# Unit 0's second half activated a place sooner, and step 3's w, v and constants loaded at other places

## The chip, the cores and the metric

The kernel runs on one core of one Trainium2 chip. The metric is device time in microseconds (us) of one execution; lower is better. TensorE (PE in the profile) does the matrix products, VectorE (DVE), ScalarE (ACT) and GpSimd (POOL) the rest, and SyncE (SP) issues most of the transfers from memory. Each engine works through its own queue in the order in which the program wrote it.

## The reference

Two blocks follow each other. The first is a linear attention with decay (batch 4, 8 heads, 768 tokens, head size 48), the second a feed-forward layer on the 3072 tokens with 384 features and 2048 hidden units, whose activation is h * erf(softplus(h)):

```python
for t in range(S):
    cur = np.einsum('bhd,bhe->bhde', u[None] * kt, vt)
    y[:, :, t] = np.einsum('bhd,bhde->bhe', rt, state + cur)
    state = wt[:, :, :, None] * state + np.einsum('bhd,bhe->bhde', kt, vt)
# x = y as (tokens, features)
h = x @ w_in
sp = np.maximum(h, 0.0) + np.log1p(np.exp(-np.abs(h)))
g = h * erf(sp)
return g @ w_out
```

The weights `w_in` and `w_out` come as 64-bit floats and are turned to 32 bits in the kernel.

## The kernel before, in words

**Steps and units.** The work is cut into 12 steps, s = 0 to 11. A step takes 128 tokens of two batches through the attention: it loads r and k (`in`), the decays (`w`) and `v`, multiplies tokens in pairs of blocks that double in size (levels 1 to LOG = 6: `level_products`, L546, makes the products, `scale`, L334, multiplies the decays in for the next level, `take_level`, L558 and L565, picks up what the level gives), and ends with `from_own` (L580), transposes of k (L919, copied by L921), the state (`state_part`, L654, L941 to L946) and `through_state` (L606). That leaves the step's 256 tokens as xT, through the PSUM tile `y` (L613, L633, L634, and rows moved by DMA in L640). From step 4 (`DIRECT`) on, the low levels come from rows instead, which `prepare` works out on VectorE and GpSimd (L469 to L490) with `u_row`, and with `block_sb` in L520.

A unit is the feed-forward work of one step's tokens. `hidden` (L1008) multiplies xT by `w_in` in two halves g = 0 and 1 of four pieces each; a piece fills one of two PSUM banks named m and ScalarE copies it to h (L1017). A half is then activated in three stages: softplus (L990) and erf (L993) on ScalarE, each with a load of its table, and the product with h (L997, two instructions on VectorE). `project` (L1040) multiplies by `w_out`, four f-blocks to a piece; it uses the same two banks.

**What sets the order.** All five queues are written out by hand under a manual schedule. In steps 1 to 3 `attend` calls `place(n)` after each level (n = 0 to 5), after the transposes (6) and at the end (7). A place does up to three things: it converts a block of weights (`convert_at`, with the table `CONVERT`), it runs some activation stages (`advance(STAGES[s][n])`), and it runs a piece or two of a unit (`beside`). In step 2 these are the eight pieces of unit 1, one to a place, after a rest of unit 0's last piece at place 0; in step 3 unit 0 is projected at places 0 to 3 (two pieces to a place) and unit 2 is multiplied at places 4 to 7.

**Activation stages.** The stages stand in one list, `later`, in the order in which the halves became complete. `advance(count)` takes stages from its front; a count of 1 is one stage, 2 is two. With the counts of the kernel before, unit 0's second half gets its softplus at place 7 of step 2, its erf at place 0 of step 3 and its product at place 1, where unit 1's first half also gets its softplus.

**Conversion of the weights.** Block i (two of the 16 f-blocks of `w_in` for i < 8, of `w_out` for i from 8 on) is loaded as two halves of 384 KB into one of three buffers `words` (L147). For `w_out`, ScalarE scales the high words into the PSUM tile `y` (L256) and the low words into `rest` (L262), VectorE shifts `y` (L271) and merges the sign (L276), and GpSimd adds `rest` (L284). A buffer is free again after L276. There is one tile `y`, which the attention uses too. The last three blocks of `w_out` (i = 13 to 15) are converted in step 3 at places 0 to 2.

**Loads.** `load_step(s + 2)` at the end of step s loads the tiles of the step after next. At the end of step 1 it issues for step 3, in this order on SyncE's queue: `in` (L147, 1 MB), `w` (L151, 512 KB), `block_sb` (L198, 32 KB), `u_row` (L199, 24 KB) and `v` (L186, 384 KB), between the weights of block 10 and of block 11. The tiles `w` and `v` have two buffers each, used in turn.

Of the kernel before, what the change touches and what calls it, by code (L numbers as in the profile page):

```python
# [39 lines left out]
DIRECT = 4  # L40
NEAR_LOG = 4
NEAR = 1 << NEAR_LOG
LOG = 6
# [18 lines left out]
def kernel(  # L62
# [14 lines left out]
    nc = tc.nc  # L77
# [40 lines left out]
    block_sb = const.tile([P, HC], FP32, name="block_sb")  # L118

    sums = const.tile([P, NEAR, NEAR], FP32, name="sums")  # L120
    u_row = const.tile([P, D], FP32, name="u_row")
# [22 lines left out]
    def load_halves(dst, src):  # L144

        for i in range(2):
            nc.sync.dma_start(out=dst[:, i], in_=src[:, i])  # L147

    def load_w(s):
        ws[s] = ins.tile([P, JP, C], FP32, name="w")  # L150
        nc.sync.dma_start(out=ws[s][:], in_=rkw[s][:, 2])  # L151
# [31 lines left out]
    def load_v(s):  # L183

        vt = loaded[s][1]
        nc.sync.dma_start(out=vt[:], in_=v[s])  # L186

    def load_step(s):
        t = ins.tile([P, 2, JP, C], FP32, name="in")
        vt = ins.tile([P, NH, D], FP32, name="v")  # L190
        if s < DIRECT:
            load_halves(t, rkw[s])
        else:
            nc.sync.dma_start(out=t[:], in_=rkw[s][:, 0:2])
        if s <= DIRECT:
            load_w(s)
        if s == 3:
            nc.sync.dma_start(out=block_sb[:], in_=block_mask)  # L198
            nc.sync.dma_start(out=u_row[:], in_=u_rows)  # L199
        loaded[s] = t, vt  # L200
        load_v(s)

    def near_log(s):
        return NEAR_LOG - (s == DIRECT)
# [3 lines left out]
    def load_rows(s):  # L208

        rk = wide.tile([P, 2, DM, 2], I32, name="words", bufs=3)  # L210
        rk = rk[:].rearrange("p x n two -> p x (n two)").bitcast(FP32)
        w = wide.tile([P, 2, DM], I32, name="rest", bufs=2)
        w = w[:].rearrange("p x n -> p (x n)").bitcast(FP32)
        nc.sync.dma_start(out=rk, in_=rk_rows[s])
        nc.sync.dma_start(out=w, in_=w_rows[s])
        rows_of[s] = [x.rearrange("p (t n) -> p t n", t=NEAR) for x in (rk[:, 0], rk[:, 1], w)]
# [370 lines left out]
    def fence():  # L587

        nc.vector.tensor_copy(
            out=seen[:].rearrange("p (e g t) -> p e g t", e=NE, g=NP),  # L590
            in_=y[:].rearrange("p e j q t -> p e (j q) t")[..., HC - 1 : HC + 1],
        )
# [95 lines left out]
    def attend_late(s, run):  # L688
# [12 lines left out]
        if before:  # L701
            from_own(before, ready[before][0], 0)
            through_state(before, xTs[before])
            if s + 1 < n_steps:
                load_step(s + 1)
# [140 lines left out]
    def stay_warm(times):  # L846

        for _ in range(times):
            ps = ps_m.tile([P, NC, P], FP32, name="m")
            nc.tensor.matmul(  # L850
                ps[:], lhsT=ident[:], rhs=ident[:, None, :].to_broadcast([P, NC, P]),
                start=True, stop=True,
            )

    def keep_busy(pp, columns=(DM, DM // 2)):

        zeros = states[1][0][:].rearrange("p n d -> p (n d)")
        for n in columns:
# [3 lines left out]
            )  # L862

    def attend(s, xT, early, place, behind):

        c, in_t, vt, made, S, S_next, ends = parts_of(s)
# [280 lines left out]
    def advance(count=None):  # L1147

        while later and count != 0:
            stage, last = later.pop(0)  # L1150
            stage()
            count = count and count - 1
            if last and not count:
                break

    def beside(s, k):


        kind, of, pieces = (projs, s - 3, 2) if k < 4 else (hids, s - 1, 2)
        if s in ALONE:  # L1160
            kind, of, pieces = hids, s - 1, 1
        for _ in range(pieces):
            piece(kind, of)
# [11 lines left out]
    def in_order(s, k):  # L1175


        order = ("APPP", "APPP", "APPHH", "AHHH", "AHHH")
        for what in order[k]:
            if what == "A":  # L1180
                advance()
            elif what == "P":
                piece(projs, s - 3)
            else:
                piece(hids, s - 1)
# [17 lines left out]
    def run_late(s, tokens, following=None):  # L1203

        for what in tokens.split():
            if what == "A":
                advance()
            elif what == "P":
                piece(projs, s - 3)
            elif what == "H":  # L1210
                piece(hids, s - 1)
            elif what == "F":
                next(following, None)
            elif what == "G":
                mixing.send(nc.gpsimd)
            elif what == "s":
                softplus_chunk()
            elif what[0] == "e":
                erf_chunk(what[1])
            elif what == "m":  # L1220
                multiply_chunk()
            elif what[0] == "k":
                to_lane(s - 2, what[1:3], what[3])
            else:
                blend(s - 2, *(int(n) for n in what[1:]))
                if what == "S3":
                    del lanes["11"], lanes["22"]
                elif what == "S4":
                    del lanes["12"]
# [6 lines left out]
    )  # L1236

    STAGES = {
        1: (0, 0, 0, 0, 0, 0, 1, 0), 2: (1, 0, 0, 0, 0, 0, 1, 1), 3: (1, 2, 1, 0, 0, 2, 1, 1)
    }  # L1240
    ALONE = {1, 2}

# [8 lines left out]
    for kk in range(KT):  # L1251
        n = D // KT
# [3 lines left out]
    with tc.manual_schedule(  # L1256
        engines={getattr(mybir.EngineType, x) for x in ("PE", "DVE", "Activation", "Pool", "SP")}
    ):
        stay_warm(6)
        for t in (*states[0], *states[1], middle):  # L1260
            nc.gpsimd.memset(t[:], 0.0)
        nc.gpsimd.memset(over_blocks[:], 1.0)
        nc.scalar.copy(u_row[:, :1], ident[:, :1])
        stages, send = convert(
            [
                (into[:, f : f + 2, :], given[:, f : f + 2, :])
                for into, given in ((w_in_sb, w_in), (w_out_sb, w_out))
                for f in range(0, NT, 2)
            ]
        )  # L1270
        stages["l"](0, loaded[0][0][:, 1, JP - 1, C - 1 : C])
        for s in range(n_steps):
            xTs[s] = xs.tile([P, KT, UNIT], FP32, name="xT")
            places = iter(range(8))

            def convert_at(n, late=True):
                if s < len(CONVERT) and n < len(CONVERT[s]):
                    send(CONVERT[s][n][late])

            def place(n):  # L1280
                if n == LOG - 1 and DIRECT - 1 <= s <= DIRECT:
                    load_rows(s + 2)
                for due in {(3, 4): (5,), (4, 3): (6,), (4, 5): (7,)}.get((s, n), ()):
                    load_w(due)
                if s >= DIRECT:
                    in_order(s, next(places))
                    return
                if s in ALONE:
                    if s == 2 and not n:

                        next(hids[0])
                        turns.pop("ahead")()
                    convert_at(n)
                    if s == 2 and not n:
                        beside(s, next(places))
                        advance(STAGES[s][n])
                        return
                    advance(STAGES[s][n])
                else:
                    advance(STAGES[s][n])  # L1300
                    convert_at(n)
                    if s == DIRECT - 1 and not n:
                        load_rows(DIRECT)
                beside(s, next(places))

            def run(n, following):
                if n == 3 and s < n_steps - 2:
                    load_rows(s + 2)
                if n == 3 and s + 3 < n_steps:
                    load_w(s + 3)  # L1310
                run_late(s, LATE.get(s, USUAL)[STAGES_LATE.index(n)], following)

            if s > DIRECT:
                attend_late(s, run)
                continue
            if s:
                attend(
                    s, xTs[s], lambda n: convert_at(n, False), place, lambda: convert_at(LOG + 2)
                )
            else:  # L1320
                attend_first(xTs[s])
            if s and s + 2 < n_steps:
                load_step(s + 2)
        s = n_steps
        from_own(s - 1, ready[s - 1][0], 1)
        fence()
        run_late(s, "s P")
        from_own(s - 1, ready[s - 1][0], 0)
        through_state(s - 1, xTs[s - 1])
        run_late(s, "m ey m P s P P ep m P P P S H H s H ey m H H s H ep m H H")  # L1330
        run_late(s + 1, "s P ey m P s P P ep m P P P S")
        run_late(s + 2, "P P P P P P P")
# [96 lines left out]
```

## Time and profile before

| what | value |
| --- | --- |
| median of 3 runs | 596.46 us (594.95 to 597.97) |
| profiled execution: its own time | 598.04 us |
| profiled execution: its span | 596.3 us |
| TensorE busy | 583.9 us (98%) |
| VectorE busy | 440.3 us (74%) |
| ScalarE busy | 361.2 us (61%) |
| GpSimd busy | 272.0 us (46%) |
| mean granted clock of TensorE | 0.997 |

The span is the time from the first to the last instruction of the profiled execution; its own time has some 1.7 us around it. In the profile, L1008 is line 1008 of the kernel, and out<-in are tiles by the program's names. "Idle before" is time in which the engine stood still ahead of an instruction, with what it waited for last. Step 1 runs from about 27 to 60 us, step 2 to 96 us, step 3 to 153 us; later steps take some 45 to 50 us each.

### The profile page before, as it was taken

What the parts mean: (1) busy time and instruction counts of PE and PEld (TensorE: products, weight loads), DVE (VectorE), ACT (ScalarE), POOL (GpSimd) and SP (SyncE); (2) the same over time, 40 slices, a digit from 0 to 9 for tenths busy, and PEclk for the clock granted to TensorE, in tenths of its full rate; (3) what the DMA queues carried; (4) which work ended last, traced back from release to release, by engine and by line L of the source; (5) the groups of instructions that cost most, each with busy time, mean ns of one, the idle gap of its engine ahead of it and who ended that gap; (6) DMA issues with size and microseconds to landing.
All of it is one profiled execution on the core that took longest, in us unless ns stands there. A gap on an engine that the chain in (4) does not pass through costs nothing.

```text
span 596.3 us, 16614 instructions
## 1 busy us (share of the span) xinstructions
PE 583.9 (98%) x7264; PEld 500.8 (84%) x7264; DVE 440.3 (74%) x518; ACT 361.2 (61%) x474; POOL 272.0 (46%) x305
## 2 busy tenths in 40 slices
PE   8899999989999999999999999999999999999997
PEld 6687777568768757898898898898898898898997
DVE  6786885998996799799799799799799525023140
ACT  3568867616534398665666666666666664746710
POOL 3456382700588559749449449459459000000000
PEclk9999999989999999999999999999999999999999
DMA  7684672341314324334334334334331300000000
GB/s 239 234 310 163 218 248 79 142 142 20 140 38 154 69 90 168 72 107 169 72 108 168 73 106 169 73 108 132 73 107 53 73 9 26 2 21 13 2 27 27
DMA packets 53937, 63.24 MB, mean 106 GB/s; under 512 B 35144, under 2 KB 40424, under 8 KB 52840
## 3 DMA queue, kind: packets, MB, share of 16 engines
q1 hardware_dynamic: 53480, 61.98, 32.5%
q8 instruction: 57, 0.93, 0.7%
q10 hardware_dynamic: 384, 0.20, 0.1%
q14 instruction: 16, 0.13, 0.1%
HBM read 52.39 MB, written 8.69 MB: 102 GB/s over the span
## 4 chain that ended last, share of the span: by engine, by line
PE 88%; DVE 5%; ACT 3%; DMA 1%; issue 1%; ACTq 0%; POOL 0%; DVEq 0%; SPq 0%; POOLq 0%
PE m L1008 39%; PE m L1116 28%; PE m L1040 8%; PE pp L546 5%; PE y L580 2%; PE pp L654 2%; DVE in L334 2%; PE y L606 2%; DMA words<-in_moe_w_out 1%; PE m L850 1%; PE pp L919 1%; DVE h L997 1%; ACT rest L262 1%; DVE own L558 1%; ACT y L256 1%
## 5 line engine op out<-in xcount | busy, mean ns | idle before, releaser
L1008 PE MATMUL m<-xT,w_in_sb 128*128 128x256 f32 x1152 | 258.6, 383 | 1.5 <-ACT h L1017 1.4
L1008 PEld LDWEIGHTS m<-xT,w_in_sb 128*128 128x128 f32 x1152 | 217.4, 191 | 33.1 <-ACT h L1017 1.6
L1017 ACT COPY h<-m 128x512 f32<-128x512 f32 x96 | 55.5, 580 | 87.5 <-PE m L1008 87.4
L334 DVE TENSOR_TENSOR in<-in,tot_sb 128x1024 f32<-128x1024 f32 (+1 forms) x59 | 82.6, 1400 | 16.4 <-PE pp L546 14.3
L469 POOL TENSOR_TENSOR rk<-words 128x528 f32<-128x528 f32 (+3 forms) x28 | 42.4, 1514 | 91.6 <-DVE sums L459 81.2
L473 POOL TENSOR_TENSOR words<-words,rest 128x528 f32<-128x528 f32 (+10 forms) x77 | 78.2, 1016 | 6.0
L1040 PE MATMUL m<-w_out_sb,h 128*128 128x384 f32 x192 | 64.3, 491 | 0.8 <-DVE h L997 0.8
L1040 PEld LDWEIGHTS m<-w_out_sb,h 128*128 128x128 f32 x192 | 35.7, 190 | 24.5 <-issue 0.9
L1116 PE MATMUL m<-mixed,h 128*128 128x192 f32 x288 | 51.1, 331 | 0.0
L1116 PE MATMUL m<-w_out_sb,h 128*128 128x192 f32 x288 | 50.3, 329 | 0.0
L964 ACT ACT_TABLE_LOAD x36 | 46.2, 1283 | 2.7 <-issue 2.0
L1116 PEld LDWEIGHTS m<-w_out_sb,h 128*128 128x128 f32 x288 | 46.9, 190 | 0.5
L1116 PEld LDWEIGHTS m<-mixed,h 128*128 128x128 f32 x288 | 46.6, 190 | 0.9
L968 ACT ACT_TABLE_LOAD x36 | 46.2, 1283 | 1.7 <-DVE room L1099 1.1
L546 PEld LDWEIGHTS pp<-in 48*64 48x64 f32 (+1 forms) x2368 | 33.4, 126 | 13.6 <-DVE in L334 6.0
L1116 PE MATMUL m<-w_out_sb,room 128*128 128x192 f32 x256 | 44.2, 326 | 0.0
L1116 PEld LDWEIGHTS m<-w_out_sb,room 128*128 128x128 f32 x256 | 42.0, 190 | 0.0
L973 DVE TENSOR_TENSOR h<-h,y 128x1024 f32<-128x1024 f32 x17 | 20.7, 1215 | 28.3 <-ACT y L968 28.2
L546 PE MATMUL pp<-in 48*64 48x64 f32 (+1 forms) x2368 | 37.7, 212 | 3.1 <-DVE in L334 3.1
L964 ACT ACTIVATE room<-h 128x1024 f32<-128x1024 f32 x36 | 38.0, 1057 | 0.4
L973 DVE TENSOR_TENSOR h<-h,pp 128x1024 f32<-128x1024 f32 x19 | 23.0, 1213 | 19.5 <-ACT pp L968 19.5
L469 POOL TENSOR_TENSOR words<-words 128x336 f32<-128x336 f32 (+6 forms) x49 | 35.3, 720 | 3.8
(141 smaller groups left out, 821.7 us busy)
## 6 DMA issues: line engine op xcount, KB each, us to landing
in<-in_rkw SPq DMA_DIRECT2D x8, 1024.0 KB, 5.4
words<-in_moe_w_in SPq DMA_DIRECT2D x16, 384.0 KB, 4.3
words<-in_moe_w_out SPq DMA_DIRECT2D x16, 384.0 KB, 3.5
words<-in_rk_rows SPq DMA_DIRECT2D x8, 768.0 KB, 5.8
w<-in_rkw SPq DMA_DIRECT2D x11, 512.0 KB, 6.9
v<-in_v SPq DMA_DIRECT2D x12, 384.0 KB, 6.3
out<-o SPq DMA_DIRECT2D x24, 192.0 KB, 2.1
in<-in_rkw SPq DMA_DIRECT2D x7, 512.0 KB, 5.3
```

What stands on the lines that cost most here:

```text
L334: nc.vector.tensor_mul(halves, halves, view(tots[level - 1], 0, [[1, n], [2, nb], [0, half]]))
L469: engine.tensor_mul(terms[n], r[:, :, n:], k[:, :, : near - n])
L473: engine.tensor_mul(k[:, :, :m], k[:, :, :m], w[:, :, n : n + m])
L546: nc.tensor.matmul(pp[s0 : s0 + m, e, n, :m], lhsT=rk[rows(e), 1, n, s0 : s0 + m], rhs=rk[rows(e), 0, n, t0 : t0 + m], start=True, stop=True,)
L580: nc.tensor.matmul(y[at(e, p), e, j, p // 2, t], lhsT=vt[t, n * NE + e, :], rhs=own[t, e * JP + n, :], start=swap == 1 and not j and not q ...
L964: nc.scalar.activation(sp_room, chunks[0], AF.Softplus)
L968: nc.scalar.activation(at, sp_room, AF.Erf)
L973: nc.vector.tensor_mul(h, h, at)
L1008: nc.tensor.matmul(ps[:, ff, :], lhsT=w_in_sb[:, g * FG + f + ff, kk * P : (kk + 1) * P], rhs=xT[:, kk, :], start=kk == 0, stop=kk == KT - 1,)
L1017: nc.scalar.copy(h[:, f : f + FT, :], ps[:])
L1040: nc.tensor.matmul(ps[j][:], lhsT=gs[g][:, f, j * C : (j + 1) * C], rhs=w_out_sb[:, g * FG + f, :], start=g + f == 0, stop=g == NG - 1 and ...
L1116: nc.tensor.matmul(to, lhsT=a[:, f], rhs=b[:, f], start=start and f == 0, stop=f == FG - 1, skip_group_check=True,)
```

## The change

The change has two parts. First, the counts of `STAGES`: place 6 of step 2 takes two stages instead of one, and place 1 of step 3 one instead of two. The first stage at place 6 is the product of unit 0's first half, as before; the second is now the softplus of unit 0's second half, ahead of the copy of the piece of that place. Its erf then comes at place 7 of step 2, ahead of the copy there, and its product at place 0 of step 3, ahead of the conversion of block 13. Unit 1's first half is activated at the same places as before. On VectorE, the two L997 instructions of that half move from behind the L558 of level 2 to behind L898 (level 1). On ScalarE, two table loads, softplus and erf move accordingly. The queues of TensorE and GpSimd keep their order.

Second, the loads for step 3 other than `in`. `w` is issued at place 5 of step 1, behind the weights of block 9. `v`, `block_sb` and `u_row`, in this order, are issued at place 4 of step 2, behind the weights of the last block. The weights of block 11 follow directly on `in` of step 3.

```diff
@@ load_step
-        if s <= DIRECT:
+        if s == DIRECT:
             load_w(s)
-        if s == 3:
-            nc.sync.dma_start(out=block_sb[:], in_=block_mask)
-            nc.sync.dma_start(out=u_row[:], in_=u_rows)
         loaded[s] = t, vt
-        load_v(s)
+        if s > 3:
+            load_v(s)
@@ STAGES
-        1: (0, 0, 0, 0, 0, 0, 1, 0), 2: (1, 0, 0, 0, 0, 0, 1, 1), 3: (1, 2, 1, 0, 0, 2, 1, 1)
+        1: (0, 0, 0, 0, 0, 0, 1, 0), 2: (1, 0, 0, 0, 0, 0, 2, 1), 3: (1, 1, 1, 0, 0, 2, 1, 1)
@@ place
                     convert_at(n)
+                    if (s, n) == (1, LOG - 1):
+                        load_w(3)
+                    if (s, n) == (2, LOG - 2):
+                        load_v(3)
+                        nc.sync.dma_start(out=block_sb[:], in_=block_mask)
+                        nc.sync.dma_start(out=u_row[:], in_=u_rows)
```

## Prediction

> **What bounds the kernel now.** I read the shares of busy time first, then TensorE's waits, then its timeline where the waits lie, then the timelines of the engines it waits for.
>
> ```profile
> PE 583.9 (98%) x7264; PEld 500.8 (84%) x7264; DVE 440.3 (74%) x518; ACT 361.2 (61%) x474; POOL 272.0 (46%) x305
> ```
>
> TensorE is busy for 583.9 of 596.3 us, so only its 12.4 us of holes, and any slow stretch in its busy time, can be won. Its waits over the whole run, those that matter (in total, times, longest):
>
> ```profile
> PE pp L546 <- DVE in L334: 3.1, 4, 2.3
> PE m L1008 <- ACT h L1017: 1.4, 2, 1.1
> PE m L1040 <- DVE h L997: 0.8, 1, 0.8
> ```
>
> After 126 us there is no wait on this list. TensorE's timeline (start, duration, idle before):
>
> ```profile
> 80.17 2.86 PE L1008 MATMUL m<-xT,w_in_sb 128*128 128x256 f32 x12 [1.08 <-ACT h L1017]
> 84.03 2.86 PE L1008 MATMUL m<-xT,w_in_sb 128*128 128x256 f32 x12 [0.32 <-ACT h L1017]
> ...
> 110.85 5.40 PE L1040 MATMUL m<-w_out_sb,h 128*128 128x384 f32 x16 [0.78 <-DVE h L997]
> ...
> 117.27 5.43 PE L1040 MATMUL m<-w_out_sb,h 128*128 128x384 f32 x16
> 125.03 1.16 PE L546 MATMUL pp<-in 48*64 48x64 f32 x64 [2.34 <-DVE in L334]
> 126.12 7.13 PE L1008 MATMUL m<-xT,w_in_sb 128*128 128x256 f32 x24
> ```
>
> Four holes lie within reach, 4.52 us: two in step 2 (s=2) behind ScalarE, two in step 3. The last row is a fifth cost: the same 24 matmuls take 5.45 us at 133.87. The table of stretches (clock in the third column from the end) shows why:
>
> ```profile
> 125.00:126.00 1.00, 0.97 (x64) 0.97 (x64) 1.00 (x2) 0.00 (x0) 0.00 (x0) 1.00 0.87 201
> 127.00:128.00 1.00, 1.00 (x4) 0.74 (x3) 0.90 (x4) 0.00 (x0) 0.00 (x0) 0.50 0.99 416
> ```
>
> Right behind the 2.34 us hole the clock is halved for some 3.3 us, which costs 7.13 - 5.45 = 1.68 us. Who makes the hole: VectorE in step 3, without idle from 103.69 on.
>
> ```profile
> 103.69 2.08 DVE L334 TENSOR_TENSOR in<-in,tot_sb 128x1024 f32<-128x1024 f32 x1 [0.97 <-PE pp L546]
> ...
> 108.71 3.97 DVE L997 TENSOR_TENSOR h<-h,room 128x1024 f32<-128x1024 f32 x2
> 112.61 1.63 DVE L334 TENSOR_TENSOR in<-in,tot_sb 128x1024 f32<-128x1024 f32 x1
> ...
> 116.61 2.26 DVE L476 TENSOR_TENSOR words<-words,u_row 128x768 f32<-128x768 f32 x1
> 118.80 1.49 DVE L469 TENSOR_TENSOR rk<-words 128x672 f32<-128x672 f32 x1
> ...
> 123.76 1.22 DVE L334 TENSOR_TENSOR in<-in,tot_sb 128x1024 f32<-128x1024 f32 x1
> ```
>
> The last of these releases TensorE at 125.03; the product of L997, 3.97 us, stands in front of it. And ScalarE, in step 2:
>
> ```profile
> 77.92 0.91 ACT L256 ACTIVATE y<-words 128x768 f32<-128x768 f32 x1 [3.22 <-DMA words<-in_moe_w_out]
> ...
> 91.74 1.28 ACT L990 ACT_TABLE_LOAD   x1
> 93.03 1.91 ACT L990 ACTIVATE room<-h 128x2048 f32<-128x2048 f32 x1
> 95.23 0.59 ACT L1017 COPY h<-m 128x512 f32<-128x512 f32 x1 [0.29 <-PE m L1008]
> ...
> 99.86 0.87 ACT L256 ACTIVATE y<-words 128x768 f32<-128x768 f32 x1 [2.36 <-DMA xT<-y]
> ```
>
> The 3.22 us wait for weights is what pushes the copies of L1017 at 79.54 and 83.39 behind TensorE.
>
> **What the Trainium skill says.** "TensorE: Matmul & The Clock Gate", Part 1, has the clock fall to half after an idle window of about 3.4 us, the window running freely. Here 2.34 us was enough, and holes of 1.08 and 0.78 us cost no clock (1.00 in both stretches). "GPSIMD Engine Reference", section 1, says that GpSimd shares its SBUF interfaces with VectorE's instructions of two SBUF inputs. The trace agrees: L334 takes 1.22 us alone and 2.08 beside an add of L284; L997 takes 2.36 alone (138.59) and 3.97 beside L284 and L408. "DMA: Bandwidth & Descriptors", section "Issuing engines are not separate DMA queues", has all transfers run on the same 16 engines, so bytes issued ahead delay what follows: 308 GB/s moved from 64 to 75 us.
>
> **The change, part by part.**
>
> *The loads of step 3.* w (512 KB), v (384), the block mask (32) and u_row (24) were issued at 66.19 to 68.75, ahead of five loads of weights. w goes to step 1, place 5, behind the weights issued up to 50.44; the engines move 5 to 7 GB/s between 55 and 62, and its buffer was last read near 33. v and the two constants go behind the last weights of step 2 (85.5 before). They are needed at 139 (L580), 151 (L520) and 116.6 (L476), and land near 90: cost nothing, with over 22 us of cover. In SyncE's queue the next after them is xT at 97.25, which waits for ScalarE anyway. What it gives: 952 KB at 308 GB/s are 3.2 us, so the weights that landed at 77.8 land near 74.6. ScalarE is then free at 74.7, but bank y only when L276 ends (74.44 + 0.95), so L256 starts near 75.4: 2.5 us sooner. The copies end near 77.6 and 81.5; TensorE asks at 79.09 and 82.63. Both holes go: 1.40 us.
>
> *The activation.* Softplus of unit 0's second half (1.28 + 1.91) moves ahead of the copy of place 6, erf (the same) ahead of the copy of place 7; no table load is added. With 1.4 us off: the L386/L389 row ends at 89.7, softplus 92.9, copy 93.4, erf 96.6, copy 97.1. TensorE wants the two banks back at 95.7 and 102.1, so 2.3 and 5 us cover it. Late next: the copy of y starts at 97.0 (94.9 if only shifted), the xT rows and step 4's loads behind it go at 100.8 instead of 99.9, and L256 starts at 97.0 + 3.56 = 100.6. xT is needed at 126. Step 4's rows (3.05 MB with in, w, v) were in by about 109.5 and so come by 110.5; L476 needs them at 112.7.
>
> *The product.* L997 now stands behind L898, at 97.1, waits for nothing (erf ends 96.6), and GpSimd is idle: 2.4 us, in VectorE's idle of 2.30 and 0.97 before 103.69. The 0.78 us wait at 110.85 goes. Queued behind it: L271/L276 start at 101.5 (wait for L256), end 103.4; L334 (level 2) ends 105.5, TensorE wants it at 107.5; L271/L276 107.3; L558 108.5; L334 (level 3) 110.3; L271/L276 112.1 (ScalarE's softplus of unit 1 and L256 end at 109.2); L558 112.7. So L476 starts at 112.7, not 116.61: 3.9 us. GpSimd then still has the rest of its totals, L284 and L926, some 4.0 us of work instead of 2.7 (1.82 + 0.84); before, that 2.7 cost VectorE (2.26 - 0.95) + (1.49 - 0.86) = 1.94, so 0.73 of it; 1.3 more cost about 0.9, rounded down to 0.7 as some is hidden in L558. L334 ends 3.2 us sooner, at 121.8. TensorE arrives at 122.70 - 1.40 - 0.78 + 0.5 (the last weights' L284 now ends near 117, wanted at 116.45) = 121.0 and waits 0.8. So at 125.03 the gain is 3.2, VectorE's, not the sum of the holes.
>
> *The clock.* A hole of 0.8 us is of the size that cost no clock, so 1.68 us more. After this VectorE is again ahead: it waits for TensorE 0.92 us at 147.12, 1.54 at 193.62 and 1.67 at 203.94. The tightest place is 171.68, wanted from L334 that ends 170.72; with VectorE 4.1 and TensorE 4.9 sooner 0.2 us are left. No wait follows, so the gain reaches the end.
>
> Sum: 598.04 - 3.2 - 1.68 = 593.1 for the profiled execution's own time. The median shown is 1.58 below that time, about the price of the halved clock; whether the median execution had it I can't see. If so, 596.46 - 4.9 = 591.6; if not, 593.3. I take 592.5 between them.
>
> **Unknown costs.** The time-sharing with GpSimd is the softest term: with none the gain at 125.03 is 3.9, with VectorE stopped for all 4.0 us 2.1. The clock is worth 0 to 1.68. Ends: 2.1 to 5.6.
>
> **Rivals.**
> 1. *The loads were hidden anyway*: weights wait for their buffers, not for bytes; ScalarE's wait stays. Against: the chain of waits runs through that transfer for 8.31 us. Then L476 starts near 114.6 and the gain is about 1.7: 594.8.
> 2. *A new wait takes the place*: GpSimd or the rows hold the chain from L476, of which only 1.0 is left: 595.4. For it: GpSimd's totals, up to 115.48 before, still run.
> 3. *Slower: ScalarE's queue.* 6.4 us now stand ahead of the copies and of L256. Place: L334 level 2, with 2 us of slack. Each us that ScalarE slips past that is one for TensorE; past 5.2 us (2 and the gain of 3.2) the kernel is slower. Two table switches and a wait on a late load could do it: a slip of 9 us gives 600. Against: every duration in the row is measured.
> 4. *No effect*: the change doesn't reach the bound, 596.5. Against: the holes stand on TensorE's own timeline.
>
> **Chances.** Forecast 0.62, rival 1 0.13, rival 2 0.10, rival 3 0.10, rival 4 0.05. What a measurement of this kernel can tell from no change is about 0.5%, 3.0 us. The forecast and a little of rival 1 (its half-clock saved too) are faster: 0.65. Rivals 1, 2 and 4 lie within: 0.25. Slower 0.10. Range: down to 590.4 (a gain of 5.6 and half a us of scatter), up to 596.3, which takes in rivals 1 and 2 and leaves out 3 and 4.
>
> **What would show it.** L256 near 75.4 with hardly a wait for weights; no wait before L1008 in step 2; L997 near 97 at 2.4 us; no wait of L1040 on L997; L476 near 113; a hole under 1.2 us before L546; clock 1.00 throughout. Wrong if L476 stays beyond 115, if L1040 waits for a copy or GpSimd for over 1 us, or if the half clock shows up elsewhere.

## The result, and the profile after

The changed kernel takes 591.82 us (median of 4 runs, 591.62 to 592.82) against 596.78 us before (median of 4 runs, 594.95 to 597.97). The ratio is 0.9923 with a 95% interval of 0.9895 to 0.9951: 0.8% faster. The profiled execution went from a span of 596.3 us to 591.0 us, 5.3 us less, and its own time from 598.04 to 592.82 us. Line numbers of the changed kernel are two lower than those of before: L1006 is L1008, L1038 is L1040, L544 is L546, L332 is L334, L995 is L997.

TensorE's waits over the whole run (in total, times, longest):

```profile
PE pp L544 <- DVE in L332: 1.0, 4, 0.3
...
PE m L1006 <- ACT o L1047: 0.6, 1, 0.6
```

Of the 2.3 us under level 5 0.3 are left, and the waits for h are gone, both for ScalarE's copy and for VectorE's product. One small wait is new behind the change (a second, 0.63 us at 6.61, lies ahead of anything that it moves). TensorE's timeline at the places shown of before:

```profile
79.34 2.86 PE L1006 MATMUL m<-xT,w_in_sb 128*128 128x256 f32 x12
...
82.81 2.86 PE L1006 MATMUL m<-xT,w_in_sb 128*128 128x256 f32 x12
...
108.78 5.43 PE L1038 MATMUL m<-w_out_sb,h 128*128 128x384 f32 x16
...
120.97 1.16 PE L544 MATMUL pp<-in 48*64 48x64 f32 x64 [0.31 <-DVE in L332]
122.06 5.45 PE L1006 MATMUL m<-xT,w_in_sb 128*128 128x256 f32 x24
```

Level 5 starts at 120.97 instead of 125.03, 4.06 us sooner. The 24 matmuls behind it take 5.45 us instead of 7.13, another 1.68 us. The table of stretches (clock in the third column from the end) has the full clock there:

```profile
122.00:127.00 5.00, 5.00 (x34) 4.37 (x24) 4.81 (x10) 0.59 (x1) 0.00 (x0) 1.00 0.95 332
```

VectorE, which set the hole before:

```profile
97.16 2.35 DVE L995 TENSOR_TENSOR h<-h,room 128x1024 f32<-128x1024 f32 x2
...
108.92 1.26 DVE L332 TENSOR_TENSOR in<-in,tot_sb 128x1024 f32<-128x1024 f32 x1 [1.54 <-PE pp L544]
...
112.57 2.24 DVE L474 TENSOR_TENSOR words<-words,u_row 128x768 f32<-128x768 f32 x1
114.73 1.48 DVE L467 TENSOR_TENSOR rk<-words 128x672 f32<-128x672 f32 x1
...
119.70 1.22 DVE L332 TENSOR_TENSOR in<-in,tot_sb 128x1024 f32<-128x1024 f32 x1
```

The product takes 2.35 us where VectorE was idle, not 3.97 in the chain. The scaling of level 3, which stood behind the product, now waits 1.54 us for TensorE: the chain hangs on TensorE again, and starts its rows (L474) at 112.57 instead of 116.61. And ScalarE in step 2:

```profile
75.71 0.92 ACT L254 ACTIVATE y<-words 128x768 f32<-128x768 f32 x1 [0.71 <-DVE w_out_sb L274]
```

It waits 0.71 us for the tile y, and no longer 3.22 us for weights.

### The profile page after: what moved, and what is told of

It reads as the page before. It is cut to its first block, busy times and chain, and to the rows that moved or that the text cites. A ratio compares the mean times of both kernels' runs of the same rounds, so it can differ in the third digit from the quotient of the medians.

```text
span 591.0 us, 16616 instructions
## 1 busy us (share of the span) xinstructions
PE 581.3 (98%) x7264; PEld 499.1 (84%) x7264; DVE 436.5 (74%) x518; ACT 361.3 (61%) x474; POOL 270.7 (46%) x305
## 4 chain that ended last, share of the span: by engine, by line
PE 89%; ACT 4%; DVE 3%; issue 2%; DMA 1%; ACTq 0%; SPq 0%; DVEq 0%
PE m L1006 42%; PE m L1114 28%; PE pp L544 6%; PE m L1038 5%; PE y L578 2%; PE pp L652 2%; PE y L604 2%; DVE in L332 1%; ACT room L962 1%; PE pp L917 1%; ACT L966 1%; DMA u_sb<-in_u 1%; ACT L962 0%; DVE rk L467 0%; ACTq L638 0%
## 5 line engine op out<-in xcount | busy, mean ns | idle before, releaser
L1006 PE MATMUL m<-xT,w_in_sb 128*128 128x256 f32 x1152 | 256.9, 381 | 0.8 <-ACT o L1047 0.6
L1006 PEld LDWEIGHTS m<-xT,w_in_sb 128*128 128x128 f32 x1152 | 216.1, 190 | 31.7 <-ACT o L1047 1.0
L1015 ACT COPY h<-m 128x512 f32<-128x512 f32 x96 | 55.7, 580 | 83.7 <-PE m L1006 83.7
L332 DVE TENSOR_TENSOR in<-in,tot_sb 128x1024 f32<-128x1024 f32 (+1 forms) x59 | 82.0, 1390 | 17.0 <-PE pp L544 14.4
L467 POOL TENSOR_TENSOR rk<-words 128x528 f32<-128x528 f32 (+3 forms) x28 | 42.5, 1517 | 92.1 <-DVE sums L457 81.7
L1038 PE MATMUL m<-w_out_sb,h 128*128 128x384 f32 x192 | 64.3, 491 | 0.0
L1038 PEld LDWEIGHTS m<-w_out_sb,h 128*128 128x128 f32 x192 | 35.7, 190 | 23.6
L544 PEld LDWEIGHTS pp<-in 48*64 48x64 f32 (+1 forms) x2368 | 33.6, 126 | 11.9 <-issue 6.5
L544 PE MATMUL pp<-in 48*64 48x64 f32 (+1 forms) x2368 | 38.0, 212 | 1.2 <-DVE in L332 1.0
L406 POOL TENSOR_TENSOR tot_sb<-tot_sb 128x256 f32<-128x256 f32 (+4 forms) x50 | 36.2, 723 | 3.8
```

Of the source, the lines that this page charges most:

```text
L332: nc.vector.tensor_mul(halves, halves, view(tots[level - 1], 0, [[1, n], [2, nb], [0, half]]))
L406: nc.gpsimd.tensor_mul(new, pair[:, :, 0], pair[:, :, 1])
L467: engine.tensor_mul(terms[n], r[:, :, n:], k[:, :, : near - n])
L544: nc.tensor.matmul(pp[s0 : s0 + m, e, n, :m], lhsT=rk[rows(e), 1, n, s0 : s0 + m], rhs=rk[rows(e), 0, n, t0 : t0 + m], start=True, stop=True,)
L1006: nc.tensor.matmul(ps[:, ff, :], lhsT=w_in_sb[:, g * FG + f + ff, kk * P : (kk + 1) * P], rhs=xT[:, kk, :], start=kk == 0, stop=kk == KT - 1,)
L1015: nc.scalar.copy(h[:, f : f + FT, :], ps[:])
```

## Experiments

### Each part alone

The loads alone: the changed kernel with the old counts.

```diff
-        ... 2: (1, 0, 0, 0, 0, 0, 2, 1), 3: (1, 1, 1, 0, 0, 2, 1, 1)
+        ... 2: (1, 0, 0, 0, 0, 0, 1, 1), 3: (1, 2, 1, 0, 0, 2, 1, 1)
```

> Only the loads of step 3 moved, the activation where it was. My theory: ScalarE's 3.22 us wait for weights shrinks to about 0.7, both holes of TensorE in step 2 go (1.40 us), everything behind shifts by that, the product stays at its old place at 3.9 us, so the hole of about 2.3 us before level 5 and the halved clock behind it stay: 1.4 us faster than before, ratio 0.9977. Rival (the loads carry most of the gain): 4 to 5 us faster, ratio 0.992. Rival (the loads were hidden anyway): no change.

Measured: ratio to the kernel before 0.9981 (0.9964 to 0.9999), median 597.05 of 22 runs against 597.81 of 43. It is what the theory said (0.9977); a ratio of 1, no change, lies just outside the interval. In its trace the wait of ScalarE for weights is gone and step 2 has no hole, but the hole before level 5 is as long as ever:

```profile
PE pp L544 <- DVE in L332: 3.1, 4, 2.3
```

The activation alone: the kernel before with the new counts.

```diff
-        ... 2: (1, 0, 0, 0, 0, 0, 1, 1), 3: (1, 2, 1, 0, 0, 2, 1, 1)
+        ... 2: (1, 0, 0, 0, 0, 0, 2, 1), 3: (1, 1, 1, 0, 0, 2, 1, 1)
```

> Only the activation moved, the loads where they were. My theory: the two holes of step 2 stay (1.40 us), the 0.78 us wait of L1040 goes, the chain from L476 starts near 114.5 instead of 116.6, so the hole before level 5 shrinks to some 1.1 us and the clock stays full: 2.0 + 1.7 = 3.7 us faster, ratio 0.9938. My rival 1 as written before the result: about 1.7 us faster, ratio 0.997 (half clock stays). If both parts are only the sum of two independent gains: this one plus the loads alone make 5.0 us.

Measured: ratio 0.9914 (0.9881 to 0.9947), median 592.86: 5.0 us faster, more than the 3.7 expected, and the interval takes in the changed kernel's 0.9923. Its trace shows two things that I hadn't expected. L476 starts at 112.64, not 114.5; and of the 1.40 us in step 2 only 0.33 us stand as a wait:

```profile
82.89 2.86 PE L1008 MATMUL m<-xT,w_in_sb 128*128 128x256 f32 x12 [0.33 <-ACT h L1017]
...
121.03 1.16 PE L546 MATMUL pp<-in 48*64 48x64 f32 x64 [0.29 <-DVE in L334]
```

The loads were all at their old places in this run, but the wait of ScalarE for the weights was shorter:

```profile
76.77 0.88 ACT L256 ACTIVATE y<-words 128x768 f32<-128x768 f32 x1 [2.25 <-DMA words<-in_moe_w_out]
```

2.25 us instead of 3.22. SyncE's issue of v took 0.53 us here and 1.01 us in the profile of before, and the weights were issued at 68.07 instead of 68.86. Up to place 6 of step 2 the two kernels are the same, so this difference is one between executions, and two traces can't tell which of the waits is the usual one. To leave out where a run starts, I take from each trace the stretch from place 1's matmuls of unit 1 (start at 70.8 to 71.6) to level 5 of step 3:

| kernel | from | to | stretch, us | less than before |
| --- | --- | --- | --- | --- |
| before | 71.26 | 125.03 | 53.77 | |
| loads alone | 71.54 | 123.35 | 51.81 | 1.96 |
| activation alone | 71.07 | 121.03 | 49.96 | 3.81 |
| both | 71.58 | 120.97 | 49.39 | 4.38 |

1.96 and 3.81 make 5.77, and both together give 4.38. But 0.97 us of the 3.81 are the shorter wait of that one execution (2.25 instead of 3.22), which the change of the activation didn't bring. An estimate without them: 2.84 and 1.96 make 4.80, 0.42 more than both. The loads alone already cut TensorE's wait for the product (L1038 on L995) from 0.78 to 0.34 us, 0.44 that the activation takes away too; this may be what is counted twice.

The runs of one series say about the same. At full clock (0.999 or 1.0) the medians are 596.55 before, 595.29 for the loads alone, 592.43 for the activation alone and 591.64 for the activation with `w` alone moved (below): gains of 1.26 and 4.12, and 4.91 together, 0.47 less than their sum. So the two gains nearly add.

### Where the product stands, or ScalarE's order

```diff
-        ... 2: (1, 0, 0, 0, 0, 0, 2, 1), 3: (1, 1, 1, 0, 0, 2, 1, 1)
+        ... 2: (1, 0, 0, 0, 0, 0, 2, 1), 3: (0, 2, 1, 0, 0, 2, 1, 1)
```

> Changed kernel, but the product of unit 0's second half put back to place 1 of step 3 (behind L556 of level 2, beside GpSimd's adds); softplus and erf stay a place sooner, loads stay moved. My theory: what counts is where VectorE does the product. It starts near 107.4, takes 3.9 us, L1038 waits for its halves some 0.8 us or more, the chain starts 3 to 4 us later and the hole of 2 us and the half clock return: 1.4 us faster than before, ratio 0.9977. Rival (it is ScalarE's order, the erf out of the row of conversions, that gives the gain): ratio 0.992 as in the changed kernel.

Measured: ratio 0.9981 (0.9964 to 0.9999), median 597.04 of 22 runs: the same as the loads alone, as the theory said. Softplus and erf a place sooner give nothing that can be measured by themselves. VectorE's timeline:

```profile
107.04 3.96 DVE L995 TENSOR_TENSOR h<-h,room 128x1024 f32<-128x1024 f32 x2
110.93 1.63 DVE L332 TENSOR_TENSOR in<-in,tot_sb 128x1024 f32<-128x1024 f32 x1
...
114.94 2.25 DVE L474 TENSOR_TENSOR words<-words,u_row 128x768 f32<-128x768 f32 x1
```

The product takes 3.96 us again, L474 starts 2.37 us later than in the changed kernel, and the hole is 2.33 us. The wait of L1038 for its halves, "0.8 us or more" in the expectation, is 0.47.

### How many of the loads

v and the constants go back ahead of the weights, only w stays moved.

```diff
+        if s == 3:
+            nc.sync.dma_start(out=block_sb[:], in_=block_mask)
+            nc.sync.dma_start(out=u_row[:], in_=u_rows)
         loaded[s] = t, vt
-        if s > 3:
-            load_v(s)
+        load_v(s)
```

(the three loads at place 4 of step 2 are dropped)

> Changed kernel with v, the block mask and u_row loaded at the end of step 1 again, ahead of the weights of block 11; only w moved. My theory counts bytes: 512 of 952 KB are gone from in front of the weights, they land 1.7 us sooner, near 76.1; TensorE needs ScalarE to start by 76.3, so both holes of step 2 still go and the time is that of the changed kernel within 0.3 us, ratio 0.992. Rival (each load counts, or SyncE's four issues of 0.4 to 1.0 us do): the words land later than 76.3, 0.3 to 0.7 us are lost, ratio 0.993.

Measured: ratio 0.9901 (0.9868 to 0.9934), median 591.95, the same as the changed kernel. ScalarE starts at 75.53 after a wait of 1.33 us for weights, TensorE has no wait in step 2, and the stretch of the table above is 49.39 us (70.77 to 120.16), to the hundredth that of the changed kernel. Moving w is enough. That bytes rather than issues count isn't shown by it: one issue fell away with the 512 KB.

### The hole and the clock

The first product of step 4's rows is done again by VectorE, once or twice more, with the same result; this lengthens the chain before level 5 and nothing else. (The two lines put in bring the line numbers behind them back to those of before.)

```diff
         nc.vector.tensor_mul(terms[0], k, u_times)
+        for _ in range(1 if near < NEAR else 0):
+            nc.vector.tensor_mul(terms[0], k, u_times)
```

> Changed kernel with the first product of step 4's rows (L474, 128x768) done once more by VectorE, same result, 0.95 us, ahead of the scaling that TensorE waits for before level 5. My theory: TensorE is bound by this chain alone there, so its hole of 0.31 us becomes 1.26 us, and a hole of that size costs no clock: 0.95 us slower than the changed kernel, ratio to the kernel before near 0.9925, clocks 1.0 in nearly all runs. Rival (any hole of over 1 us halves the clock): 2.6 us slower, ratio 0.995, clocks 0.997. Rival (VectorE has slack there): no loss.

Measured: ratio 0.9924 (0.9892 to 0.9956), median 593.06 of 7 runs. In TensorE's timeline:

```profile
121.49 1.16 PE L546 MATMUL pp<-in 48*64 48x64 f32 x64 [1.19 <-DVE in L332]
122.58 5.45 PE L1008 MATMUL m<-xT,w_in_sb 128*128 128x256 f32 x24
```

The hole is 1.19 us and the matmuls behind it keep 5.45 us. Five of the 7 runs have a clock of 0.999 or 1.0.

> The same with two repeats (1.9 us): the hole becomes 2.2 us, as long as that of the kernel before. My theory: the halved clock comes from the length of this hole, so it returns in about three of four runs as in the kernel before: 1.9 us and some 1.7 us more where it strikes, 3 to 3.6 us slower than the changed kernel, ratio to the kernel before near 0.996, with clocks 0.997 or 0.994 in most runs. Rival (the half clock has another cause than the hole, such as the product or the loads at their old places): 1.9 us slower, clocks 1.0.

Measured: ratio 0.9959 (0.9945 to 0.9973), median 595.24 of 20 runs, 3.4 us over the changed kernel. TensorE's timeline:

```profile
122.22 1.48 PE L546 MATMUL pp<-in 48*64 48x64 f32 x64 [2.24 <-DVE in L332]
123.62 6.75 PE L1008 MATMUL m<-xT,w_in_sb 128*128 128x256 f32 x24
```

And its table of stretches:

```profile
123.00:126.00 3.00, 3.00 (x34) 2.43 (x27) 2.79 (x8) 0.00 (x0) 0.00 (x0) 0.50 1.01 389
```

With product and loads at their new places and the hole alone restored to 2.24 us, the half clock is back. Sixteen of the 20 runs show a mean clock of 0.997 or 0.994. So it comes with the hole, not with the old places. A mean clock below 0.999 is read here as at least one stretch of half clock; where it lay can be seen in the profiled runs alone. The mean clock of a run falls in steps, and the runs of the kernel before (81 of these two series) sort by it:

| mean clock of the run | runs of before | their median, us |
| --- | --- | --- |
| 1.0 | 19 | 596.52 |
| 0.996 to 0.997 | 37 | 597.76 |
| 0.994 | 19 | 599.00 |
| 0.991 | 6 | 602.29 |

One step, 0.003 of some 596 us, is 1.8 us of clock lost, or 3.6 us at half clock; the profile showed 3.3. In these medians each of the first two steps costs 1.24 us, less than the 1.68 of the profiled execution. In the profiled run of the loads alone, with 0.994, the half clock holds for about twice as long, 1.99 and 7.83 us for two rows that take 1.16 and 5.45:

```profile
124.00:130.00 6.00, 6.00 (x63) 4.98 (x56) 5.79 (x11) 0.00 (x0) 0.00 (x0) 0.50 0.66 261
```

Of the runs with the short hole (changed kernel 4, activation alone 6, w alone 6, the last experiment 6) 19 of 22 have a clock of 0.999 or 1.0.

### ScalarE's cover

Softplus of unit 0's second half is done three times, which puts 3.8 us more in front of ScalarE's copies.

```diff
-                nc.scalar.activation(held[0], h[:], AF.Softplus)
+                for _ in range(3 if rooms["next"] == 2 else 1):
+                    nc.scalar.activation(held[0], h[:], AF.Softplus)
```

> Changed kernel with the softplus of unit 0's second half done three times at place 6 of step 2, same result, 3.8 us more of ScalarE ahead of the copies and of the conversion of block 13. It measures my rival 3. My theory by the trace of the changed kernel: the bank that L1038 wants at 95.9 comes back at 97.4 (1.5 us of wait), the conversions go 3.8 us later, L474 starts near 115.4 instead of 112.6, the hole before level 5 is 1.7 us: 2.9 us slower than the changed kernel, and up to 1.7 more where the clock halves; ratio to the kernel before 0.996 to 0.998. Rival (ScalarE has that much cover): under 0.5 us, ratio 0.992. Rival (each us costs a us): 3.8 us or more.

Measured: ratio 0.9967 (0.9943 to 0.999), median 595.37 of 12 runs. The 9 of them at full clock have a median of 595.09, 3.3 us over the changed kernel, 2.9 expected; the other three show a clock of 0.994. In the trace level 5 comes 3.06 us later (the stretch of the table above is 52.45). The size is right, and one of the two waits is where I expected it (one line was put in, so L1039 and L1016 are L1038 and L1015 of the changed kernel):

```profile
PE m L1039 <- ACT h L1016: 1.7, 1, 1.7
PE m L1039 <- POOL w_out_sb L282: 1.3, 1, 1.3
...
PE pp L544 <- DVE in L332: 0.6, 3, 0.2
```

The bank of L1038 comes 1.66 us late, as worked out. The rest isn't a hole before level 5 but a wait for the last block of weights, which GpSimd adds too late for place 3. The chain behind VectorE costs 0.2 us at most.

### The new wait

```diff
-        by_scalar = {(kk, 1) for kk in range(KT) if s <= DIRECT}
+        by_scalar = {(kk, 1) for kk in range(KT) if s < DIRECT}
```

> Changed kernel with all six xT rows of step 4 issued by SyncE instead of three by ScalarE. In the trace of the changed kernel ScalarE's three issues at 198.2 take 2.8 us and a copy of o ends 0.57 us too late for TensorE at 224.31, a wait the kernel before had not. My theory: that is where 0.5 us of the gain were given back; ScalarE comes 2 us sooner, the wait goes, 0.5 us faster than the changed kernel, ratio to the kernel before about 0.991. Rival (the wait comes only with a slow issue and most runs don't have it): no difference. Rival (SyncE's six issues push step 6's loads 2.5 us back and something waits): slower.

Measured: ratio 0.9909 (0.9876 to 0.9942), median 591.88 of 6 runs, no different from the changed kernel. The wait of 0.57 us isn't there, but neither is it in the traces of the activation alone, of w alone and of the two holes, which left ScalarE's issues alone. With ScalarE's cover tried above it is 0.34 us. The two traces that have it are those with the slowest issues: ScalarE's three took 2.76 us in the changed kernel and 2.53 with ScalarE's cover tried, and 2.12 to 2.34 in the other seven in which ScalarE issues them. So the rival holds. No version here is clearly faster than the changed kernel: the intervals of w alone and of this one take in its 0.9923.

## Why the prediction was right, point by point

**The bound.** TensorE's own holes and the slow stretch behind them were all that could be won, and they were won: 4.06 us at level 5, and the clock.

**The loads.** In the two profiled executions they did what was said: ScalarE starts at 75.71 (forecast 75.4), and the 1.40 us are gone. The base of this term was weak, one execution with a wait of 3.22 us. In the trace of the activation alone 0.33 us of the 1.40 stood as a wait and some 0.2 as a later start at 79.02, so between these two traces the loads are worth 0.57 us. Rival 1 had more to it than I gave it. In the changed kernel SyncE, done with `in` at 66.39, waited until L274 had freed a buffer at 67.44, and issued the weights at 67.52, 1.34 us sooner than before and not by the whole time of the moved loads. ScalarE's wait for them does go. That the transfers were all but idle between 55 and 62 is so; the trace has 2 GB/s there, not 5 to 7.

**The product.** It stood at 97.16 for 2.35 us (forecast 97.1, 2.4), L474 at 112.57 (112.7). The second of these is in part luck. I had VectorE at work without a wait from 101.5 up to level 3, with its scalings slowed to 2.08 and 1.63 us by GpSimd. They took 1.22 and 1.26 us, so VectorE was early at level 3, waited 1.54 us for TensorE, and came out at the same time. That the place of the product and not that of the erf counts is shown by the product put back.

**Time-sharing with GpSimd.** This term was mis-sized. I added 0.7 us because GpSimd would still be at its totals beside L474. L474 and L467 took 2.24 and 1.48 us, as before (2.26 and 1.49), so the chain ended 4.06 us sooner, the value I had kept as the upper bound (3.9). What I missed is that the totals suffer from the product as the product does from them. GpSimd's totals of before and, below, of the changed kernel:

```profile
109.57 2.03 POOL L408 TENSOR_TENSOR tot_sb<-w 128x512 f32<-128x512 f32 x1
111.68 3.80 POOL L408 TENSOR_TENSOR tot_sb<-tot_sb 128x256 f32<-128x256 f32 x5
```

```profile
108.04 1.05 POOL L406 TENSOR_TENSOR tot_sb<-w 128x512 f32<-128x512 f32 x1
109.17 2.94 POOL L406 TENSOR_TENSOR tot_sb<-tot_sb 128x256 f32<-128x256 f32 x5
```

With the product gone, GpSimd ran them in 1.05 + 2.94 us, not 2.03 + 3.80, and ended its last add at 113.99, not near 117; with the product put back they took 2.03 + 3.79 again. Beside L474 there was only the work of before (L282 and L924), none of the 1.3 us that I had added. The 0.5 us wait that I gave TensorE there didn't come either, and the hole is 0.31, not 0.8.

**The clock.** Right, and tried. Of 81 runs of the kernel before 62 show a clock of 0.997 or less, so most executions had the half clock; whether the one of 596.46 us had it isn't on record. The measured 591.82 lies by the reading that took it so (591.6); 592.5, taken between the two, was 0.7 too high.

**The reach to the end.** Nearly right: 5.75 us were won by 203 us (202.76 to 197.01 for step 5's first products), of which one slow issue took back 0.57 in the profiled execution. I had named 171.68 as the tightest place and missed that one, where the copy of o came 0.06 us ahead of TensorE in the profile of before.

**The sum.** 4.9 us were forecast against the profiled execution's own time, 3.2 at level 5 and 1.68 for the clock, and 5.2 measured: 4.06 and 1.68, less the 0.57 of the new wait. The total came closer than its terms: 0.9 too little for the chain and 0.6 too much for a wait put at nothing lie on opposite sides, which is luck.

**The rivals.** The slower one was tried. I had given it 2 us of slack at level 2, by which 3.8 us of slip would have cost 1.8; they cost 3.1 in the trace. So the cover is some 0.7 us, and the place was wrong: the loss came at the bank of L1038 and at the last weights, not at level 2. In the changed kernel no such slip was seen. A wait for GpSimd, as rival 2 feared, appeared only there.

## What to carry to other kernels

A product that needs nothing new belongs where its engine idles. Here that brought level 5 2.5 us sooner than with the product put back (stretches of 51.92 and 49.39 us), which is less than its own 3.97, and spared most runs the half clock behind the hole; GpSimd, which had worked beside it, got faster too. Measure two gains each alone and both, and in runs of the same clock: from one trace each they seemed to overlap by 1.4 us, of which most was one execution's shorter wait. A hole that is followed by slower matmuls costs more than its length, and a single profile can't tell how often that happens; the clocks of many runs can.

## What the runs showed of the hardware that I hadn't expected

**A longer hole brought the half clock more often.** Holes of 0.29 to 0.32 us left 19 of 22 runs at full clock, one of 1.19 us 5 of 7, one of 2.24 us 4 of 20, and the kernel before with its 2.34 us 19 of 81. The loads alone and the product put back, with 2.33 to 2.34 us, left 9 of 44, and ScalarE's cover tried, with holes of 1.66 and 1.31 us, 9 of 12. So few runs can't tell a hole of 1.2 us from one of 0.3; 2.2 us stand out. The Trainium skill, "TensorE: Matmul & The Clock Gate", Part 1, speaks of an idle window of some 3.4 us; here 2.2 us are enough in most runs. The traces show one such stretch or one twice as long; mean clocks of 0.991 would be three. All these holes lie in step 3, and why the same hole costs some executions the clock and others not stays open.

**Of VectorE and GpSimd the one that started first kept its pace.** In the kernel before, GpSimd's add (L284) starts at 102.86, ahead of the scaling of level 2:

```profile
102.86 1.82 POOL L284 TENSOR_TENSOR w_out_sb<-w_out_sb,rest 128x768 int32<-128x768 int32 x1 [8.65 <-DVE w_out_sb L276]
```

It takes 1.82 us, and VectorE's scaling at 103.69 2.08. In the changed kernel the scaling starts first, at 103.04, and takes 1.22; the add is the one that is held up:

```profile
103.26 2.67 POOL L282 TENSOR_TENSOR w_out_sb<-w_out_sb,rest 128x768 int32<-128x768 int32 x1 [10.27 <-DVE w_out_sb L274]
```

The trace of the activation alone has the same (1.22 and 2.67 us). That is seen in these pairs and wasn't tried on its own. If it holds, a change of order on one of the two engines can shift the delay to the other without any of it vanishing.
